# Six slots for streamed weights, other streamed pieces, and a row copied by one engine, in a recurrent memory transformer

## The chip, the cores and the metric

The kernel runs on one core of a Trainium2 chip. The metric is the device time of one execution in microseconds, as the median of several runs. A profiled execution gives a trace of every instruction and transfer; L448 is line 448 of the kernel file.

## The reference

Two independent parts are computed in bfloat16 and written side by side.

```python
def _A_ref(x, wqkv, wo):          # S = 2048, D = 640, 32 heads of 20
    ...                           # attention of each token to 8 tokens, 2 apart
def _B_ref(x, mem0, Wq, Wk, Wv, Wo, seg_len):
    ...                           # Dm = 640, H = 32, Dh = 192, M = 8, seg_len = 32
    for s in range(n_seg):        # 64 segments
        h = jnp.concatenate([mem, xs], axis=1)        # 8 + 32 = 40 rows
        q = jnp.einsum('btd,dhe->bhte', h, Wq)        # k, v the same
        ...
        p = _softmax(scores, axis=-1)
        o = jnp.einsum('bhqk,bhke->bhqe', p, v)
        o = jnp.einsum('bhte,hed->btd', o, Wo)
        mem = o[:, :M, :].copy()
        outs.append(o[:, M:, :])
```

In part B the first 8 rows of a segment's output are the memory of the next segment, so the 64 segments run one after the other.

## The kernel before

Part A runs first, for some 178 us. The text below is about part B.

**Weights in pieces.** Each of Wq, Wk and Wv is cut into 4 groups of 8 heads (1536 columns) and 5 chunks of 128 rows: a piece is named (group, chunk) and has 384 KB. Wo is cut into 24 output pieces of 320 KB, six to a group. Most pieces are resident in SBUF. Those listed in STREAMED (L258) are loaded anew in each segment: first copied to DRAM in a fitting layout (copy_streamed, L295), then, at each use, loaded by get_unit (L377) into one of `nbuf` slots of a rotating pool (wstream, 5 slots of 3072 bytes a partition). All these loads are issued by SP in the program's order. A load waits until TensorE has done the last matmul on the piece that was in its slot, that is, `nbuf` streamed pieces earlier. `pre` and `early` (L330, L363) say which resident pieces are loaded before, near the end of, and after part A.

**A segment** (L602) has a written order of TensorE's work: projections of Q and K by group, each followed by turns (transposes by a matmul with the identity, L465), scores (L521), softmax on VectorE and ScalarE (L526 to L538), values, mixing (L572), and the output projection (L586) that sums all heads into one PSUM tile Y. Rows of the next segments that are known beforehand are projected together with the present ones in some segments (RENEW, L261): a group's K or V pieces then get 8 matmuls each for 4.

**The order of a segment's pieces** as TensorE uses them: Q0, K0, Q1, K1, Q2, V0, K2, V1, output pieces 0 to 5, Q3, K3, V2, output 6 to 11, V3, output 12 to 17, three chunks of the late Q, output 18 to 23, two chunks of the late Q.

**The end of a segment** (L648 to L660): when Y is whole, `halves` (L458) copies its two halves to the bfloat16 tile `row`, the first by ScalarE (L459), the second by VectorE (L460). Both write one tile. TensorE finishes the late Q, whose result `halves` copies in the same way, turns the 8 memory rows (memory_rows, L590) from `row`, VectorE writes them into HX, the next segment's input (L600), and TensorE turns the late Q. The next segment's first projection reads HX. GpSimd stores `row` to the output (L659). The tile `row` shares its one buffer with the softmax tile t1 (L527) of the next segment.

`evacuate` (L426), which copies all other PSUM results, takes ScalarE and VectorE in turn.

Of the kernel before, what the change touches and what calls it, by code (L numbers as in the profile page):

```python
# [23 lines left out]
def part_a(ctx, tc, A_x, A_wqkv, A_wo, out, ident, emit_loads):  # L24
# [209 lines left out]
    with tc.manual_schedule(engines={mybir.EngineType.PE, mybir.EngineType.DVE, mybir.EngineType.Activation}):  # L234
# [5 lines left out]
        for b in range(n_blk):  # L240
# [14 lines left out]

STREAMED = {"k": ((0, 4), (0, 4), (0, 3), (0, 3)), "v": ((0, 1), (1,), (2,), (2,)),  # L258
            "o": (0, 4, 6, 8, 11, 14, 17, 18, 22, 23)}
SLOT = 1536  # L260
RENEW = {0: ("k0", "v2"), 1: ("k1", "v3"), 2: ("k2", "v0"), 3: ("k3", "v1")}  # L261
BLOCKS = 18
# [9 lines left out]
def part_b(ctx, tc, B_x, B_mem0, B_Wq, B_Wk, B_Wv, B_Wo, out, ident, n_seg, pre, nbuf, mid):  # L272
    nc = tc.nc
# [21 lines left out]
    def copy_streamed():  # L295
# [3 lines left out]
        for m, g in order:  # L299
            if m == "o":  # L300
                units += [("o", i, 0) for i in range(6 * g, 6 * g + 6) if i in STREAMED["o"]]
            else:
                units += [(m, g, dc) for dc in range(5) if m != "q" and dc in STREAMED[m][g]]
        for u in units:
# [6 lines left out]
    for m, g in need:  # L311
        if m == "o":
            resident += [("o", i, 0) for i in range(6 * g, 6 * g + 6) if i not in STREAMED["o"]]
        else:
            resident += [(m, g, dc) for dc in range(5) if m == "q" or dc not in STREAMED[m][g]]
    res, wait = {}, set()
# [113 lines left out]
    def load_x(s):  # L430
        if s < n_seg:
            nc.sync.dma_start_transpose(HXs[s % 2][:], XW[s])
# [4 lines left out]
    def ahead(s):  # L437
        return HXs[s % 2][:, :, SEG:2 * SEG]
# [16 lines left out]
        evacuate(sb[:], p[:])  # L455
        return sb

    def halves(dst, src, n):  # L458
        nc.scalar.copy(dst[:, 0:n], src[:, 0:n])  # L459
        nc.vector.tensor_copy(dst[:, n:], src[:, n:])  # L460

    def turn(sb):
        pt = ps_x.tile([128, 3, 4, 32], FP32, tag="x")
        for c in range(3):
            nc.tensor.matmul(pt[:, c], lhsT=sb[:, 128 * c:128 * c + 128], rhs=ident, start=True, stop=True)  # L465
        return pt
# [24 lines left out]
    def project_qk(s, m, g):  # L491
        renew = s == 0 or f"{m}{g}" in RENEW[s % 4]
        Xs = [ahead(s), main(s)] if renew else [main(s)]
        sbs = [to_sb(p) for p in project32(Xs, m, g)]

        def turns():
            if renew:
                turn_late(sbs[0], m, g, s, s)
            else:
                b = late.pop((m, g, s))  # L500
                fill(nc.gpsimd.tensor_copy, m, 32, L, b[:])
                free.append(b)
            fill(evacuate, m, 0, 32, turn(sbs[-1])[:])

        return turns

    def values(s, g):
        renew = s == 0 or f"v{g}" in RENEW[s % 4]
        ps = project32([ahead(s), main(s)] if renew else [main(s)], "v", g)
        for t, p in ((LV[g], ps[0]), (Vst, ps[-1]))[0 if renew else 1:]:  # L510
            v = t[:].rearrange("p (n e) -> p n e", e=64)
            w = bass.AP(v.tensor, v.offset, [v.ap[0], [256, 2], [1, 192]])
            evacuate(w, p[:].rearrange("p (h e) -> p h e", h=2))

    def scores(g):
        Sps = ps_x.tile([128, 4, L], FP32, tag="x")
        for n in range(8):
            a, part = n // 2, n % 2
            for g2 in range(2):
                at = L * (3 * a + g2 + part)  # L520
                nc.tensor.matmul(Sps[64 * g2:64 * g2 + 64, a, :], lhsT=QT[:, at:at + 64],  # L521
                                 rhs=KT[:, a, ((0, 1), (3, 2))[g2][part], :], start=(n == 0), stop=(n == 7),
                                 tile_position=(0, 64 * g2))
        return Sps

    def softmax(Sps):  # L526
        t1 = one.tile([128, 4, L], FP32, tag="t1")  # L527
        nc.vector.scalar_tensor_tensor(out=t1[:], in0=Sps[:], scalar=scale,  # L528
                                       in1=mask[:].unsqueeze(1).to_broadcast([128, 4, L]),
                                       op0=ALU.mult, op1=ALU.add)  # L530
        mx = small.tile([128, 4], FP32, tag="mx")
        nc.vector.tensor_reduce(out=mx[:], in_=t1[:], axis=AX.X, op=ALU.max)
        nc.vector.tensor_tensor(t1[:], t1[:], mx[:].unsqueeze(2).to_broadcast([128, 4, L]), op=ALU.subtract)  # L533
        nc.scalar.activation(t1[:], t1[:], ACTF.Exp)  # L534
        sm = small.tile([128, 4], FP32, tag="sm")
        nc.vector.tensor_reduce(out=sm[:], in_=t1[:], axis=AX.X, op=ALU.add)  # L536
        nc.vector.reciprocal(sm[:], sm[:])
        return t1, sm  # L538

    def put_p(s, g, t1, sm):  # L540
        i = s % 4
        if g == 0 and s:
            old = M * ((s - 1) % 4)
            nc.gpsimd.memset(P[:, 1, :, old:old + M], 0.0)
        for k, lo, hi, at in ((0, 0, 32, 0), (1, 32, L, M * i)):
            nc.vector.tensor_tensor(out=P[:, k, :, at:at + hi - lo], in0=t1[:, :, lo:hi],  # L546
                                    in1=sm[:].unsqueeze(2).to_broadcast([128, 4, hi - lo]), op=ALU.mult)

    def turn_p(split=1):

        pt = ps_x.tile([128, 2, 128], FP32 if split > 1 else BF16, tag="x")
        for late in range(2):
            src = P[:, late].rearrange("p a n -> p (a n)")
            if split == 1:
                nc.tensor.transpose(pt[:, late, :], src, ident)
                continue
            for h in range(2):
                nc.tensor.matmul(pt[64 * h:64 * h + 64, late, :], lhsT=src[:, 64 * h:64 * h + 64], rhs=ident,
                                 start=True, stop=True, tile_position=(0, 64 * h))
        PT = one.tile([128, 2, 2, L], BF16, tag="PT")  # L560
        evacuate(PT[:], pt[:].rearrange("p l (h n) -> p l h n", h=2)[:, :, :, 0:L])
        return PT
# [39 lines left out]
    def segment(s):  # L602
        last = s + 1 == n_seg
        load_x(s + 1)
        tq, tk, PT = {}, {}, {}
        tq[0] = project_qk(s, "q", 0)
        tk[0] = project_qk(s, "k", 0)
        tq[1] = project_qk(s, "q", 1)
        tq[0]()
        tk[0]()  # L610
        tk[1] = project_qk(s, "k", 1)
        put_p(s, 0, *softmax(scores(0)))
        tq[1]()
        tk[1]()
        tq[2] = project_qk(s, "q", 2)
        values(s, 0)
        soft = softmax(scores(1))
        tq[2]()
        PT[0] = turn_p()
        put_p(s, 1, *soft)  # L620
        tk[2] = project_qk(s, "k", 2)
        mix(0, PT[0])
        values(s, 1)
        tk[2]()
        PT[1] = turn_p()
        Y = ps_y.tile([128, 320], FP32, tag="y")
        project_out(Y, 0)
        put_p(s, 2, *softmax(scores(2)))
        tq[3] = project_qk(s, "q", 3)
        tk[3] = project_qk(s, "k", 3)  # L630
        mix(1, PT[1])
        values(s, 2)
        tq[3]()
        tk[3]()
        PT[2] = turn_p()
        project_out(Y, 1, range(0, 4))
        put_p(s, 3, *softmax(scores(3)))
        project_out(Y, 1, range(4, 6))
        mix(2, PT[2])
        values(s, 3)  # L640
        project_out(Y, 2, range(0, 4))
        PT[3] = turn_p(2)
        project_out(Y, 2, range(4, 6))
        mix(3, PT[3])
        if not last:
            gl = (s + 1) % 4
            ql = project32([ahead(s + 1)], "q", gl, range(0, 3))
        project_out(Y, 3)  # L648
        row = one.tile([128, 4, L], FP32, tag="t1")
        Ysb = row[:].rearrange("p a n -> p (a n)").bitcast(BF16)  # L650
        halves(Ysb, Y[:], 160)
        if not last:
            project32([ahead(s + 1)], "q", gl, range(3, 5), ql)
            sb = qk_sb.tile([128, 384], BF16, tag="sb", name="sb")
            halves(sb[:], ql[0][:], 192)
            memory_rows(s, Ysb)
            turn_late(sb, "q", gl, s, s + 1)
        for gv in range(2):
            nc.gpsimd.dma_start(out2[SEG * s:SEG * s + SEG, Dm + 320 * gv:Dm + 320 * gv + 320],  # L659
                                Ysb[64 * gv + M:64 * gv + L, :])  # L660
# [3 lines left out]
    with tc.manual_schedule(engines={mybir.EngineType.PE}):  # L664
        for s in range(n_seg):
            segment(s)


def run_all(ctx, tc, A_x, A_wqkv, A_wo, B_x, B_mem0, B_Wq, B_Wk, B_Wv, B_Wo, out, ident):
    n_seg = B_x.shape[1] // 32  # L670

    def mid(emit_loads):
        with ExitStack() as actx:
            part_a(actx, tc, A_x, A_wqkv, A_wo, out, ident, emit_loads)

    part_b(ctx, tc, B_x, B_mem0, B_Wq, B_Wk, B_Wv, B_Wo, out, ident, n_seg=n_seg, pre=110000, nbuf=5,
           mid=mid)


# [57 lines left out]
```

## Time and profile before

| what | us |
|---|---|
| median of 3 runs (2024.0 to 2032.36) | 2024.52 |
| the profiled execution | 2021.62 |
| its span, first to last instruction | 2019.8 |
| PE (TensorE matmul) busy | 1899.0 |
| DVE (VectorE) busy | 1226.9 |
| ACT (ScalarE) busy | 777.0 |

A line of groups names the line, engine, operation, the tiles written and read, the shape, the count, then busy time and mean ns of one. A line of waits names who waited for whom, the us in total, how often, and the longest. A line of windows has the stretch, its length, busy time with count of PE, PEld (weight loads), DVE, ACT and POOL, then the granted TensorE clock as a share of full speed, the DMA engines' mean busy share, and GB/s. A line of the timeline has start, length, engine, line and tiles, and in brackets the idle time before it with what ended that. SPq is the queue of SyncE, which issues transfers.

### The profile page before, as it was taken

The numbers are of one execution on the slowest core, as the hardware profiler recorded it, in microseconds if no ns is written. First come the engines' busy times: TensorE is split into PE (matmuls) and PEld (weight loads), VectorE is DVE, ScalarE is ACT, GpSimd is POOL, SyncE is SP. The second block draws the span as 40 slices with busy tenths as digits, with TensorE's granted clock in tenths as the row PEclk, the third lists the DMA queues.
The fourth block names the chain that finished last, engine by engine and source line by source line (L and its number), as shares of the span: only waits on it lengthen the run. The fifth ranks groups of instructions, "written<-read, shape, count | busy, mean of one in ns | idle before, by whom it ended". The sixth has DMA issues, their size and how long they took to land.

```text
span 2019.8 us, 98671 instructions
## 1 busy us (share of the span) xinstructions
PE 1899.0 (94%) x42640; PEld 1210.0 (60%) x42640; DVE 1226.9 (61%) x4041; ACT 777.0 (38%) x2480; POOL 259.3 (13%) x1058
## 2 busy tenths in 40 slices
PE   7998999999999999999999999999999999999998
PEld 3655566666666666566666565566655665556665
DVE  4876566655665656665566556555665565556565
ACT  3544333333333333333333333333333333334333
POOL 2000111111111111111111111111111111111111
PEclk9999999999999999999999999999999999999999
DMA  9927999999999999999899999999999998999997
GB/s 346 305 63 269 316 303 309 308 302 311 296 309 305 309 306 297 306 301 313 277 310 311 302 304 296 301 301 308 294 304 297 304 291 285 296 283 304 294 312 262
DMA packets 270134, 596.38 MB, mean 295 GB/s; under 512 B 61065, under 2 KB 72841, under 8 KB 269385
## 3 DMA queue, kind: packets, MB, share of 16 engines
q1 hardware_dynamic: 264770, 585.97, 88.0%
q8 instruction: 334, 5.47, 1.1%
q0 software_dynamic: 4928, 4.11, 0.6%
q14 instruction: 102, 0.84, 0.1%
HBM read 576.85 MB, written 18.87 MB: 295 GB/s over the span
## 4 chain that ended last, share of the span: by engine, by line
PE 55%; DMA 24%; DVE 15%; issue 3%; ACT 3%; SPq 0%; POOL 0%; DVEq 0%; ACTq 0%; POOLq 0%
PE acc L448 24%; PE Y L586 14%; DMA t<-wcopy_o 10%; DMA t<-wcopy_k 8%; PE pt L465 4%; PE pq L95 3%; PE Sps L521 3%; DMA out_dram<-row 3%; DMA t<-wcopy_v 2%; PE OTps L572 2%; DVE sb L428 2%; PE po L161 1%; DVE P L546 1%; DVE QT L428 1%; DVE sm L536 1%
## 5 line engine op out<-in xcount | busy, mean ns | idle before, releaser
L448 PEld LDWEIGHTS <-HX 128*32 128x32 bf16 x19380 | 466.2, 96 | 283.4 <-issue 50.6
L586 PEld LDWEIGHTS <-OT 128*64 128x64 bf16 x6144 | 319.8, 110 | 143.9 <-ACT OT L428 41.0
L586 PE MATMUL Y<-wres_o,OT 128*64 128x320 bf16 x3584 | 340.4, 300 | 4.1 <-ACT OT L428 1.3
L448 PE MATMUL acc<-wres_q,HX 128*32 128x384 bf16 x6460 | 335.8, 330 | 0.9 <-issue 0.3
L448 PE MATMUL acc<-t,HX 128*32 128x384 bf16 x4200 | 309.8, 329 | 15.1 <-DMA t<-wcopy_k 9.4
L586 PE MATMUL Y<-t,OT 128*64 128x320 bf16 x2560 | 280.9, 303 | 21.9 <-DMA t<-wcopy_o 20.3
L448 PE MATMUL acc<-wres_v,HX 128*32 128x384 bf16 x4844 | 277.0, 328 | 0.6 <-DVE OT L428 0.6
L448 PE MATMUL acc<-wres_k,HX 128*32 128x384 bf16 x3876 | 226.4, 328 | 0.6 <-issue 0.6
L428 DVE CAST sb<-acc 128x384 bf16<-128x384 f32 x291 | 160.9, 553 | 103.6 <-PE acc L448 87.1
L534 ACT ACTIVATE t<-t 128x160 f32<-128x160 f32 x256 | 86.2, 337 | 342.8 <-DVE t L533 341.0
L465 PE MATMUL pt<-ident,sb 128*128 128x128 bf16 x1938 | 190.5, 221 | 9.8 <-DVE sb L428 4.2
L428 ACT CAST sb<-acc 128x384 bf16<-128x384 f32 x292 | 138.8, 475 | 143.3 <-PE acc L448 136.3
L428 ACT CAST KT<-pt 64x128 bf16<-64x128 f32 (+3 forms) x517 | 139.3, 277 | 112.9 <-DVE KT L428 72.3
L465 PEld LDWEIGHTS <-sb 128*128 128x128 bf16 x1938 | 113.2, 97 | 89.6 <-issue 36.8
L528 DVE SCALAR_TENSOR_TENSOR t<-Sps,mask 128x160 f32<-128x160 f32 x256 | 82.9, 324 | 125.5 <-PE Sps L521 105.6
L428 ACT CAST OT<-OTps 128x120 bf16<-128x120 f32 x512 | 106.9, 261 | 126.5 <-PE OTps L572 125.0
L428 DVE CAST OT<-OTps 128x120 bf16<-128x120 f32 x512 | 125.5, 271 | 47.6 <-PE OTps L572 47.1
L428 DVE CAST KT<-pt 64x128 bf16<-64x128 f32 (+2 forms) x452 | 134.2, 300 | 31.1 <-ACT KT L428 23.0
L478 POOL COPY KT<-Lb 64x32 bf16<-64x32 bf16 x189 | 41.4, 219 | 825.1 <-PE Sps L521 825.1
L521 PEld LDWEIGHTS <-QT 128*64 128x64 bf16 x4096 | 100.3, 112 | 59.4 <-issue 50.3
L428 ACT CAST Vst<-acc 128x384 bf16<-128x384 f32 x205 | 98.7, 481 | 95.6 <-PE acc L448 92.0
L521 PE MATMUL Sps<-KT,QT 128*64 128x40 bf16 x4096 | 117.6, 187 | 9.2 <-DVE KT L428 6.2
(86 smaller groups left out, 1982.3 us busy)
## 6 DMA issues: line engine op xcount, KB each, us to landing
t<-wcopy_o SPq DMA_DIRECT2D x640, 320.0 KB, 4.3
t<-wcopy_k SPq DMA_DIRECT2D x512, 384.0 KB, 5.0
t<-wcopy_v SPq DMA_DIRECT2D x320, 384.0 KB, 4.8
wres_q<-in_B_Wq_dram SPq DMA_DIRECT2D x20, 384.0 KB, 7.7
wres_v<-in_B_Wv_dram SPq DMA_DIRECT2D x15, 384.0 KB, 7.7
wres_k<-in_B_Wk_dram SPq DMA_DIRECT2D x12, 384.0 KB, 7.7
wres_o<-in_B_Wo_dram SPq DMA_DIRECT2D x14, 320.0 KB, 7.6
wcopy_o<-in_B_Wo_dram SPq DMA_DIRECT2D x10, 320.0 KB, 9.4
```

The costliest lines, as they stand in the source:

```text
L95: nc.tensor.matmul(pq[32 * d:32 * d + 32], lhsT=wcol[:, k, t, 4 * c + d, :], rhs=xTs[s][:, k, :], start=(k == 0), stop=(k == 4), tile_posi ...
L161: nc.tensor.matmul(po[:, c % 2, :], lhsT=ident, rhs=prod[:, w, :], start=(w == 0), stop=(w == W - 1))
L428: (nc.scalar.copy if copies["n"] % 2 else nc.vector.tensor_copy)(dst, src)
L448: nc.tensor.matmul(ps[n][32 * j:32 * j + 32, :], lhsT=X[:, dc, :], rhs=w[:, 384 * j:384 * j + 384], start=(dc == 0), stop=(dc == 4), tile_ ...
L465: nc.tensor.matmul(pt[:, c], lhsT=sb[:, 128 * c:128 * c + 128], rhs=ident, start=True, stop=True)
L478: copy(KT[64:128, :, 3, n0:n1], src[64:128, 1])
L521: nc.tensor.matmul(Sps[64 * g2:64 * g2 + 64, a, :], lhsT=QT[:, at:at + 64], rhs=KT[:, a, ((0, 1), (3, 2))[g2][part], :], start=(n == 0), s ...
L528: nc.vector.scalar_tensor_tensor(out=t1[:], in0=Sps[:], scalar=scale, in1=mask[:].unsqueeze(1).to_broadcast([128, 4, L]), op0=ALU.mult, op ...
L534: nc.scalar.activation(t1[:], t1[:], ACTF.Exp)
L536: nc.vector.tensor_reduce(out=sm[:], in_=t1[:], axis=AX.X, op=ALU.add)
L572: nc.tensor.matmul(ps[a][:, k, :], lhsT=V[32 * a:32 * a + 32, col:col + 128], rhs=PT[32 * a:32 * a + 32, late, half, :], start=(n == 0), s ...
L586: nc.tensor.matmul(Y[64 * gv:64 * gv + 64, :], lhsT=OT[:, L * c:L * c + 64], rhs=w[:, n:n + 320], start=(i == 0 and r == 0), stop=(i == 23 ...
```

## The change

Six slots stand for five. The lists of streamed pieces are new: as many K and output pieces as before, and six V pieces for five. The resident set is smaller by that V piece, as the pool of slots is larger by one. `halves` is gone; ScalarE copies Y, and the late Q, each in one instruction.

```diff
-STREAMED = {"k": ((0, 4), (0, 4), (0, 3), (0, 3)), "v": ((0, 1), (1,), (2,), (2,)),
-            "o": (0, 4, 6, 8, 11, 14, 17, 18, 22, 23)}
+STREAMED = {"k": ((2, 4), (2, 4), (0, 4), (0, 4)), "v": ((0, 4), (0, 4), (2,), (2,)),
+            "o": (3, 5, 7, 10, 11, 13, 17, 18, 22, 23)}
...
-    def halves(dst, src, n):
-        nc.scalar.copy(dst[:, 0:n], src[:, 0:n])
-        nc.vector.tensor_copy(dst[:, n:], src[:, n:])
...
-        halves(Ysb, Y[:], 160)
+        nc.scalar.copy(Ysb, Y[:])
...
-            halves(sb[:], ql[0][:], 192)
+            nc.scalar.copy(sb[:], ql[0][:])
...
-    part_b(ctx, tc, B_x, B_mem0, B_Wq, B_Wk, B_Wv, B_Wo, out, ident, n_seg=n_seg, pre=110000, nbuf=5,
+    part_b(ctx, tc, B_x, B_mem0, B_Wq, B_Wk, B_Wv, B_Wo, out, ident, n_seg=n_seg, pre=110000, nbuf=6,
```

The orders of instructions on TensorE, VectorE, ScalarE and GpSimd stay as they are, but for the copies named and the tiles that hold a piece. On SP the 64 added loads come in, the transposing load of HX stands one streamed load later, and at the start of part B the first six streamed loads go ahead of the early resident pieces.

## Prediction

> **What bounds the kernel now.** I read the page first: shares of the span, the chain that ended last, the transfers.
>
> ```profile
> span 2019.8 us, 98671 instructions
> ...
> PE 1899.0 (94%) x42640; PEld 1210.0 (60%) x42640; DVE 1226.9 (61%) x4041; ACT 777.0 (38%) x2480; POOL 259.3 (13%) x1058
> ...
> PE 55%; DMA 24%; DVE 15%; issue 3%; ACT 3%; SPq 0%; POOL 0%; DVEq 0%; ACTq 0%; POOLq 0%
> ...
> L428 ACT CAST sb<-acc 128x384 bf16<-128x384 f32 x292 | 138.8, 475 | 143.3 <-PE acc L448 136.3
> ...
> L428 ACT CAST OT<-OTps 128x120 bf16<-128x120 f32 x512 | 106.9, 261 | 126.5 <-PE OTps L572 125.0
> ...
> t<-wcopy_o SPq DMA_DIRECT2D x640, 320.0 KB, 4.3
> t<-wcopy_k SPq DMA_DIRECT2D x512, 384.0 KB, 5.0
> t<-wcopy_v SPq DMA_DIRECT2D x320, 384.0 KB, 4.8
> ```
>
> TensorE is busy 94% of the span, so at most 120 us can be won by letting it wait less. The chain goes through streamed weights for a quarter of the span: DMA is TensorE's partner at the limit. Per segment 10 + 8 + 5 = 23 pieces are streamed (640, 512 and 320 over 64 segments). Next I asked what TensorE waits for, then what the SP queue, which starts these transfers, waits for.
>
> ```profile
> PE Y L586 <- DMA t<-wcopy_o: 20.3, 41, 1.5
> PE pt L597 <- DVE row L460: 19.9, 63, 0.4
> PE acc L448 <- DMA t<-wcopy_k: 9.4, 22, 1.4
> ...
> PE acc L448 <- DMA t<-wcopy_v: 2.7, 7, 0.6
> ```
>
> ```profile
> SPq L394 <- PE acc L448: 681.7, 771, 4.0
> SPq L394 <- PE Y L586: 279.0, 352, 2.5
> ```
>
> TensorE waits 32.4 us (70 times, mean 0.46) for streamed pieces, and 19.9 us for the row. SP in its turn spends 961 us in these two rows alone waiting until TensorE gives a slot back. Transfers thus start late for want of a slot. Is DMA also full? The windows of the trace compare the loading phase, where transfers are issued without slots, with two ordinary segments:
>
> ```profile
> 20.00:30.00 10.00, 10.00 (x188) 6.79 (x180) 3.67 (x3) 4.71 (x9) 0.00 (x0) 1.00 1.03 406
> ...
> 780.00:837.00 57.00, 54.77 (x1276) 34.94 (x1273) 34.47 (x122) 21.42 (x72) 7.64 (x32) 1.00 0.93 302
> ```
>
> The last column is GB/s: 406 there, 302 here. The column before it, DMA's busy share, is near 1 in both, so it doesn't tell how much more could be moved; GB/s does.
>
> The length of a segment comes from the transposes of the memory rows, one set per segment, first and last start in the row: (1988.6 - 218.9) / 62 = 28.54 us.
>
> ```profile
> L597 PE MATMUL pt<-ident,row x378: 166/173/194, 218.9 to 1988.6; 128*128 128x8 bf16 x126, 128*64 128x8 bf16 x63
> ```
>
> **Change 1: slots and pieces.** The new lists stream 8 K, 6 V and 10 output pieces: the added one is a V piece. A segment then moves 14 x 384 + 10 x 320 = 8576 KB (8.78 MB) for 8192; the extra 384 KB take 0.97 us of DMA at 406 GB/s. SP issues one more transfer, and it waits most of the time as it is.
>
> What a slot allows is its cycle. Five slots and 23 pieces: each slot is filled once in 28.54 x 5 / 23 = 6.20 us. Six and 24, at a segment of 27.8: 6.95 us. From issue to landing of a piece:
>
> ```profile
> DMA to landing us min/median/max: 2.9/4.7/7.9
> ```
>
> So 1.50 us is left for waiting in the slot and being read, and 2.25 after: 0.75 more on average. Placement decides where the slack is short. Prices for counting it, from the chain in order of time in one segment:
>
> ```profile
> 900.07 1.74 PE acc L448 x40
> 901.81 0.36 PE Sps L521 x16
> ...
> 908.59 1.75 PE Y L586 x24
> ```
>
> A projection piece of four matmuls is 0.17 us, an output piece 0.29, scores 0.36. In the old order, output piece 11 takes the slot of K piece (3, 0), five pieces back. Between them lie four pieces of K 3 (0.70), mix, five pieces of V 2 (0.87), turns, output pieces 6 to 10 (1.46) and scores, about 4 us: under the median landing. In the new order its slot is that of output piece 5; scores 2 and the five pieces of Q 3 come in addition (+0.36 and +0.87), so 5.2. The tightest place is now V piece (3, 2), six back from which stands K (3, 0): the old 4 us, output 11, mix and two pieces of V 3, about 4.9. Everywhere the distance is at or above the median landing; before, it wasn't.
>
> Price of a wait: besides the idle time that the view shows, it loses the overlap of matmuls. One lasts 299 ns, while 24 of them go by in 1.75 us, 73 ns each; 0.23 us per wait, so 32.4 + 70 x 0.23 = 48.5 us.
>
> ```profile
> L586 PE MATMUL Y<-t,OT x2560: 296/299/323, 198.4 to 2014.2; 128*64 128x320 bf16 x197
> ```
>
> How much of it goes? Bounds: all 48.5, or nothing, if the sixth transfer only queues behind the five. With waits of 0.46 us on average I take them as exponentially spread. The 0.75 us shrink where pieces are queued back to back, since the sixth lands 0.97 us behind the fifth; I take 0.45 net. What stays is exp(-0.45 / 0.46) = 38%, so **30 us** go.
>
> **The clock.** The last output piece, 23, has the longest waits, and they come where TensorE soon waits for the row as well. Three windows of 3.4 us before and at such a place, and the wait in the first:
>
> ```profile
> 978.60:982.00 3.40, 1.98 (x33) 0.96 (x36) 0.87 (x4) 0.85 (x3) 0.90 (x2) 1.00 0.84 309
> 982.00:985.40 3.40, 3.40 (x51) 1.77 (x47) 0.49 (x2) 0.72 (x2) 0.36 (x2) 0.50 0.90 296
> ...
> 1787.50:1790.90 3.40, 3.39 (x43) 1.64 (x47) 0.92 (x4) 0.96 (x3) 1.25 (x3) 0.51 1.02 389
> ...
> 1876.30:1879.70 3.40, 3.40 (x48) 1.81 (x44) 0.99 (x3) 0.72 (x2) 0.00 (x0) 0.50 0.98 356
> ```
>
> ```profile
> 979.66 0.46 PE L586 MATMUL Y<-t,OT 128*64 128x320 bf16 x4 [1.29 <-DMA t<-wcopy_o]
> ```
>
> The seventh column is the granted clock: 0.5 for 3.4 us, three times, 1.7 us each. Piece 23 took the slot of V piece (3, 2) and now takes that of output piece 11, a mix and three V pieces (0.52) earlier, so I let these go: **5 us** (bounds 0 and 5). The Trainium skill, "TensorE: Matmul & The Clock Gate", section Part 1, has the clock fall to half after an idle window of about 3.4 us; a wait of 1.3 us would cost no clock then, and this term would be nothing. In the trace the clock fell after 3.4 us in which TensorE was busy for 1.98, so I keep the 5.
>
> **Change 2: the row and the late Q by ScalarE alone.** The end of an ordinary segment in order of time:
>
> ```profile
> 866.96 0.29 ACT L459 CAST row<-Y 128x160 bf16<-128x160 f32 x1 [2.38 <-PE Y L586]
> 867.29 0.33 DVE L460 CAST row<-Y 128x160 bf16<-128x160 f32 x1 [2.67 <-ACT row L459]
> 867.42 0.32 ACT L459 CAST sb<-acc 128x192 bf16<-128x192 f32 x1 [0.16 <-PE acc L448]
> 867.67 0.38 PE L597 MATMUL pt<-ident,row 128*64 128x8 bf16 x6 [0.30 <-DVE row L460]
> 867.77 0.36 DVE L460 CAST sb<-acc 128x192 bf16<-128x192 f32 x1 [0.15 <-ACT sb L459]
> 867.91 0.56 PE L465 MATMUL pt<-ident,sb 128*128 128x128 bf16 x3
> 868.09 0.20 DVE L600 CAST HX<-pt 128x40 bf16<-128x40 f32 x1
> 868.40 1.00 PE L448 MATMUL acc<-wres_q,HX 128*32 128x384 bf16 x20
> ```
>
> The halves don't run side by side: VectorE's starts when ScalarE's has ended, so the row takes 866.96 to 867.62, 0.66 us. One ScalarE copy of 320 columns lies between 261 ns (120) and 475 (384): 0.42. The transposes start at 867.44 for 867.67, which their wait of 0.30 allows; HX is written by 868.06 for 868.29. The late Q is copied behind the row, 867.41 to 867.89 (475 ns), and its three turns follow at 867.94, done in time for the next projection at 868.17 for 868.40. That is 0.23 us in each of 63 segments, **14.5 us**. If the longer copy of Q held up the turns by 0.1, it would be 8; above, no more than the wait of 19.9. ScalarE, busy 38%, hides the extra; what is late next is the copy into HX.
>
> **Change 3: the start.** In the changed kernel's order of issue six streamed pieces go ahead of the last nine early resident pieces, and four stores of part A stand before these.
>
> ```profile
> 163.64 2.00 SPq L394 DMA_DIRECT2D t<-wcopy_k  x4
> 165.68 0.76 SPq L394 DMA_DIRECT2D t<-wcopy_v  x1
> 169.44 9.52 SPq L176 DMA_DIRECT2D out_dram<-ob  x4
> 179.33 1.50 SPq L328 DMA_DIRECT2D wres_v<-in_B_Wv_dram  x1
> ```
>
> Before, one early piece was behind the stores that end at 178.96; now five are, four more or 3.9 us of DMA inside segment 0. One streamed piece is earlier, and that segment lasts 39 us with its doubled projections, so most is hidden: I take **1 us lost** (bounds 0 and 4).
>
> **Sum.** 30 + 5 + 14.5 - 1 = 48.5 us. The profiled execution took 2021.62 us (its span 2019.8 and 1.8 around it), so it would take 1973.1. The median of the three runs shown, 2024.52, lies 2.9 above that execution, and the changed kernel will be measured by such a median: 1976.
>
> **Rivals.**
> All waits go: 18.5 more and the start costs nothing: 1956. For it speaks that 0.75 us exceed the mean wait; against it, landings of up to 7.9 us.
>
> The store of the row takes over. The next segment's first softmax writes into the row's buffer, so it waits for that store:
>
> ```profile
>   DMA out_dram<-row: 9.2, 11
> ```
>
> Waits for K pieces early in a segment then only turn into this one. With half of the 30 us lost that way or to the new clusters: 1991.
>
> The sixth slot does nothing, the added piece eating it: 14.5 - 1, so 2011, about no gain.
>
> The other side: DMA is full at 302 GB/s, as its share of 0.93 would have it. Then 8.78 MB take 29.1 us, 0.53 over today's segment, 63 times 33 us, less the row's 14.5 and plus the start: 2044. It decides as soon as the sustained rate is under 8.78 MB / 28.54 us = 308 GB/s. The 406 speaks against it, the share for it. The Trainium skill, "DMA: Bandwidth & Descriptors", section Bandwidth, puts the limit of HBM for one core at about 358 GB/s; by that a segment needs 24.5 us of transfers, an estimate, and the rival fails too. The trace's 406 lies above that figure.
>
> **How the numbers follow.** Forecast 0.46, all gone 0.20, half 0.18, nothing from the slot 0.08, DMA full 0.08. The range from 1948 to 2012 holds the forecast, the third case, four fifths of the second and half of the fourth, 0.84; its low end is 8 us under the second case, for waits shorter than the lost overlap, which no view of waits shows. A measurement can tell about 0.5%, 10 us, from no change: under 2014 is faster. The first three cases are faster, and 0.03 of the fourth: 0.87. Same are the rest of the fourth and 0.01 of the last, 0.06; slower is the rest of the last, 0.07.
>
> **What would show it.** In the changed profile: TensorE's waits for streamed pieces near 12 us instead of 32.4; landings about as now, near 5; the row's wait near 0.1 us each time; no half clock around piece 23; segments of 27.8 us; over 310 GB/s. Landing medians of 6 and more would mean that DMA is full; waits for the row's store well over 9 us would mean the second rival.

## The result and the profile after

The changed kernel takes 1999.64 us (median of 4 runs, 1996.27 to 2006.95), the kernel before 2028.44 (4 runs, 2024.0 to 2033.85): a ratio of 0.9862, 95% interval 0.9818 to 0.9905. A second measurement (e5 below) gave 0.9897 (0.9869 to 0.9925). The gain is thus some 20 to 29 us, about half of the 48.5 that were forecast, and inside the range. The profiled executions are 2021.62 us before and 2006.95 after, 14.7 apart; the latter is the slowest of its four, so what the two traces show in single terms is read against 14.7.

From the page of the changed kernel: span, busy time, chain, transfers.

```profile
span 2005.2 us, 98676 instructions
...
PE 1896.5 (95%) x42640; PEld 1211.5 (60%) x42640; DVE 1184.5 (59%) x3914; ACT 794.9 (40%) x2480; POOL 259.0 (13%) x1058
...
PE 60%; DMA 16%; DVE 15%; issue 4%; ACT 4%; POOL 1%; SPq 0%; DVEq 0%; ACTq 0%; POOLq 0%
...
t<-wcopy_o SPq DMA_DIRECT2D x640, 320.0 KB, 4.7
t<-wcopy_k SPq DMA_DIRECT2D x512, 384.0 KB, 5.3
t<-wcopy_v SPq DMA_DIRECT2D x384, 384.0 KB, 5.4
```

DMA's share of the chain falls from 24% to 16%. The median landing of each kind is up by 0.3 to 0.6 us: six transfers are under way where five were. The window of two segments that the prediction showed with 302 GB/s is now:

```profile
780.00:837.00 57.00, 53.63 (x1258) 34.33 (x1255) 33.08 (x118) 21.05 (x71) 7.74 (x32) 1.00 0.98 314
```

The chain by line shows the one DMA term that grew, the store of the row; before, then after:

```profile
PE acc L448 24%; PE Y L586 14%; DMA t<-wcopy_o 10%; DMA t<-wcopy_k 8%; PE pt L465 4%; PE pq L95 3%; PE Sps L521 3%; DMA out_dram<-row 3%; DMA t<-wcopy_v 2%; PE OTps L572 2%; DVE sb L428 2%; PE po L161 1%; DVE P L546 1%; DVE QT L428 1%; DVE sm L536 1%
PE acc L448 24%; PE Y L582 18%; DMA out_dram<-row 7%; PE pt L461 4%; PE pq L95 3%; DMA t<-wcopy_o 3%; DMA t<-wcopy_k 3%; PE OTps L568 3%; PE Sps L517 3%; DVE sb L428 2%; DMA t<-wcopy_v 2%; DVE t L524 2%; DVE P L542 2%; PE po L161 1%; DVE mx L528 1%
```

What TensorE waits for, in the changed kernel:

```profile
PE Sps L517 <- DVE KT L428: 11.3, 30, 0.5
...
PE acc L448 <- issue: 7.3, 13, 1.8
PE Y L582 <- DMA t<-wcopy_o: 6.8, 12, 2.0
...
PE acc L448 <- DMA t<-wcopy_k: 4.2, 9, 1.2
PE OTps L568 <- issue: 3.0, 6, 0.9
PE acc L448 <- DMA t<-wcopy_v: 3.0, 5, 1.4
...
PE Y L582 <- issue: 0.9, 1, 0.9
...
PE pt L461 <- issue: 0.3, 1, 0.3
```

Streamed pieces now cost 14.0 us in 26 waits for 32.4 in 70, and the wait for the row is gone from the view. New is "issue", time in which TensorE waits for nothing that the profile shows: 11.5 us in 21 waits. Before it was 1.6. The waits for VectorE's copies of K, the first line, have grown as well:

```profile
PE Sps L521 <- DVE KT L428: 6.2, 16, 0.4
...
PE acc L448 <- issue: 0.9, 2, 0.6
PE OTps L572 <- issue: 0.5, 1, 0.5
...
PE pt L465 <- issue: 0.2, 1, 0.2
```

The tile of softmax and streamed weights, in the changed kernel: VectorE's waits for the row's store (us, times; 9.2 and 11 before), and the landings.

```profile
  DMA out_dram<-row: 19.9, 18
...
DMA to landing us min/median/max: 3.2/5.1/7.7
```

The end of a segment, changed kernel, in order of time:

```profile
866.56 0.43 ACT L647 CAST row<-Y 128x320 bf16<-128x320 f32 x1 [2.04 <-PE Y L582]
867.01 0.48 ACT L651 CAST sb<-acc 128x384 bf16<-128x384 f32 x1
...
867.04 0.39 PE L593 MATMUL pt<-ident,row 128*64 128x8 bf16 x6
...
867.46 0.20 DVE L596 CAST HX<-pt 128x40 bf16<-128x40 f32 x1 [2.91 <-PE pt L593]
...
867.55 0.34 PE L461 MATMUL pt<-ident,sb 128*128 128x128 bf16 x3
...
867.82 0.67 PE L448 MATMUL acc<-wres_q,HX 128*32 128x384 bf16 x12
```

From the row's copy to the next projection it is 1.26 us, before 1.44 (866.96 to 868.40): 0.18 less; over all 63 segments the medians are 1.26 and 1.43. The copy of the row takes 0.43, and HX is written by 867.66; it is now the three turns of the late Q, which wait for its whole copy, that end last.

The memory rows' transposes, with the first segment's end at 221.9 (218.9 before):

```profile
L593 PE MATMUL pt<-ident,row x378: 166/173/193, 221.9 to 1973.4; 128*128 128x8 bf16 x126, 128*64 128x8 bf16 x63
```

A segment takes (1973.4 - 221.9) / 62 = 28.25 us, where 27.8 was forecast and 28.54 was the time before.

### The profile page after: what moved, and what is told of

Its sections match the earlier page's. It is cut to its first block, busy times and chain, and to the rows that moved or that the text cites. A ratio compares the mean times of both kernels' runs of the same rounds, so it can differ in the third digit from the quotient of the medians.

```text
span 2005.2 us, 98676 instructions
## 1 busy us (share of the span) xinstructions
PE 1896.5 (95%) x42640; PEld 1211.5 (60%) x42640; DVE 1184.5 (59%) x3914; ACT 794.9 (40%) x2480; POOL 259.0 (13%) x1058
## 4 chain that ended last, share of the span: by engine, by line
PE 60%; DMA 16%; DVE 15%; issue 4%; ACT 4%; POOL 1%; SPq 0%; DVEq 0%; ACTq 0%; POOLq 0%
PE acc L448 24%; PE Y L582 18%; DMA out_dram<-row 7%; PE pt L461 4%; PE pq L95 3%; DMA t<-wcopy_o 3%; DMA t<-wcopy_k 3%; PE OTps L568 3%; PE Sps L517 3%; DVE sb L428 2%; DMA t<-wcopy_v 2%; DVE t L524 2%; DVE P L542 2%; PE po L161 1%; DVE mx L528 1%
## 5 line engine op out<-in xcount | busy, mean ns | idle before, releaser
L448 PE MATMUL acc<-t,HX 128*32 128x384 bf16 x4524 | 346.1, 328 | 10.5 <-DMA t<-wcopy_k 4.2
L582 PE MATMUL Y<-wres_o,OT 128*64 128x320 bf16 x3584 | 332.6, 303 | 2.9 <-ACT OT L428 0.3
L582 PE MATMUL Y<-t,OT 128*64 128x320 bf16 x2560 | 268.5, 302 | 8.6 <-DMA t<-wcopy_o 6.8
L448 PE MATMUL acc<-wres_v,HX 128*32 128x384 bf16 x4520 | 254.3, 328 | 5.1 <-issue 4.0
L461 PE MATMUL pt<-ident,sb 128*128 128x128 bf16 x1938 | 179.6, 222 | 14.7 <-DVE sb L428 4.8
L517 PE MATMUL Sps<-KT,QT 128*64 128x40 bf16 x4096 | 120.9, 187 | 16.1 <-DVE KT L428 11.3
```

The costliest lines, as they stand in the source:

```text
L448: nc.tensor.matmul(ps[n][32 * j:32 * j + 32, :], lhsT=X[:, dc, :], rhs=w[:, 384 * j:384 * j + 384], start=(dc == 0), stop=(dc == 4), tile_ ...
L582: nc.tensor.matmul(Y[64 * gv:64 * gv + 64, :], lhsT=OT[:, L * c:L * c + 64], rhs=w[:, n:n + 320], start=(i == 0 and r == 0), stop=(i == 23 ...
```

## The experiments

Three readings were to be told apart: that the terms of the forecast hold and something new eats the rest; that the added V piece and its traffic eat it; that the row's term is worth less than 14.5 us.

### e1: the row alone

```diff
-STREAMED = {"k": ((2, 4), (2, 4), (0, 4), (0, 4)), "v": ((0, 4), (0, 4), (2,), (2,)),
-            "o": (3, 5, 7, 10, 11, 13, 17, 18, 22, 23)}
+STREAMED = {"k": ((0, 4), (0, 4), (0, 3), (0, 3)), "v": ((0, 1), (1,), (2,), (2,)),
+            "o": (0, 4, 6, 8, 11, 14, 17, 18, 22, 23)}
...
-    part_b(ctx, tc, B_x, B_mem0, B_Wq, B_Wk, B_Wv, B_Wo, out, ident, n_seg=n_seg, pre=110000, nbuf=6,
+    part_b(ctx, tc, B_x, B_mem0, B_Wq, B_Wk, B_Wv, B_Wo, out, ident, n_seg=n_seg, pre=110000, nbuf=5,
```

> Five slots and the old list of pieces, with only the row and the late Q copied by ScalarE alone. The part's own worth: the prediction had 0.23 us per segment, 14.5 us in all; in the trace of the changed kernel the stretch from the last output piece to the next segment's first projection is 0.18 us shorter (1.60 for 1.77), so this theory expects 11 us under the kernel before. Rival: with five slots an earlier segment start only makes TensorE wait longer for the first K pieces, so less than 4 us are left.

Measured: a ratio of 0.9983 (0.9959 to 1.0007), 3.4 us under the kernel before, by the interval anything from nothing to 8 us: the 11 us of the theory are excluded, and the rival fits. The end of a segment is as much shorter as in the changed kernel, but TensorE's waits are:

```profile
PE Y L582 <- DMA t<-wcopy_o: 25.9, 45, 1.4
PE acc L448 <- DMA t<-wcopy_k: 15.9, 33, 1.7
...
PE acc L448 <- DMA t<-wcopy_v: 4.2, 9, 0.9
```

46.0 us in 87 waits for 32.4 in 70. With five slots a TensorE that is ready sooner waits longer: the waits grew by 13.6 us, more than the 11 that the end of the segments gives. So the rate at which slots come round seems to set the pace.

### e2: slots and list alone

```diff
-        nc.scalar.copy(Ysb, Y[:])
+        halves(Ysb, Y[:], 160)
...
-            nc.scalar.copy(sb[:], ql[0][:])
+            halves(sb[:], ql[0][:], 192)
```

> Six slots and the new list, but row and late Q still copied in two halves. If the parts add up, the changed kernel's gain of 29 us less the row's 11: 18 us under the kernel before. Rival: the row's gain is only there because the pieces are on time; then the slots alone give nearly all, 25 us or more.

Measured: 0.9944 (0.9920 to 0.9968), 11.3 us. Neither number fits well; it is below both. Between this and the changed kernel's two ratios lie 10 to 17 us, the worth of the row when there are six slots, for 3.4 with five. That the two parts need each other is likely by this, not shown: the intervals are wide, and the profiled executions don't have the difference (spans of 2005.5 us here, 2005.2 and 2005.7 in the changed kernel's two).

### e3: the new list with five slots

```diff
-    part_b(ctx, tc, B_x, B_mem0, B_Wq, B_Wk, B_Wv, B_Wo, out, ident, n_seg=n_seg, pre=110000, nbuf=6,
+    part_b(ctx, tc, B_x, B_mem0, B_Wq, B_Wk, B_Wv, B_Wo, out, ident, n_seg=n_seg, pre=110000, nbuf=5,
```

> The changed kernel with five slots: the new list with its added piece, without the sixth slot. A slot's cycle falls from 28.54 x 5 / 23 = 6.20 us to 5.95, so TensorE waits for streamed pieces more than the kernel before's 32 us, some 50, and the time is 5 to 25 us above the kernel before in spite of the row. Rival: the new places do the work and the slot little; then the time is near the changed kernel's, 20 us or more under the kernel before.

Measured: 1.0227 (1.0191 to 1.0262), 46 us slower than before, more than expected. TensorE's waits for streamed pieces are 72.5 us in 161:

```profile
PE Y L582 <- DMA t<-wcopy_o: 32.9, 76, 1.1
PE acc L448 <- DMA t<-wcopy_k: 21.3, 46, 1.3
PE acc L448 <- DMA t<-wcopy_v: 18.3, 39, 2.1
```

The median landing was 4.7 us as in the kernel before, so DMA wasn't slower. It is the slot that makes the gain. The list by itself brings none; how much of its loss is the added piece and how much the places, this run doesn't tell.

### e4: the old list with six slots

```diff
+ALIAS = {('v', 3, 4): ('v', 3, 3)}
...
+    resident = [u for u in resident if u not in ALIAS]
...
     def get_unit(u):
+        u = ALIAS.get(u, u)
```

> Six slots with the old list of 23 pieces; the space comes from V piece (3, 4), which is not loaded: chunk 3's weights are used twice. If the added piece and its 25 MB of traffic ate part of the gain (later landings, a later store of the row, late instructions), this is 8 to 20 us faster than the changed kernel, 37 to 49 us under the kernel before, with landings near 4.7 us. Rival: the added traffic costs nothing and the missing gain has another cause; then it is within 5 us of the changed kernel.

Measured: 0.9782 (0.9747 to 0.9817), 44 us under the kernel before. Waits for streamed pieces are 5.6 us in 15. The added piece, which the smaller resident set makes necessary, and the places that go with it cost 16 to 23 us of what the sixth slot gives (0.9782 for 0.9862 and 0.9897). But "issue" stays, 12.6 us in 18 waits, and so does the store, 22.8 us: these two don't come from the added piece alone.

### e5: the changed kernel again

> The changed kernel once more, beside the next three on the same chip. If the six slots are what lets the row's 11 us through (alone the row gave 3), it lies 20 to 33 us under the kernel before, and its trace again has some 10 us of TensorE waits that nothing in the profile explains ('issue') and some 20 us of VectorE waits for the row's store. Rival: its first four runs were lucky and the parts simply add up; then 11 to 18 us under the kernel before.

Measured: 0.9897 (0.9869 to 0.9925), 20.8 us, at the lower end; "issue" 11.3 us, the store 20.5 us.

### e6: six pieces less to stream

```diff
-STREAMED = {"k": ((2, 4), (2, 4), (0, 4), (0, 4)), "v": ((0, 4), (0, 4), (2,), (2,)),
-            "o": (3, 5, 7, 10, 11, 13, 17, 18, 22, 23)}
+STREAMED = {"k": ((2,), (2,), (0,), (0,)), "v": ((0, 4), (0,), (2,), (2,)),
+            "o": (3, 5, 7, 10, 13, 17, 18, 22, 23)}
+ALIAS = {("v",1,4):("v",1,3), ("k",0,4):("k",0,3), ("k",1,4):("k",1,3), ("k",2,4):("k",2,3), ("k",3,4):("k",3,3), ("o",11,0):("o",9,0)}
```

> The changed kernel with six streamed pieces (chunk 4 of every K group and of V 1, output piece 11) neither streamed nor loaded; a resident neighbour's weights are used twice. TensorE runs the same instructions, DMA moves 2.2 MB per segment less, some 240 GB/s. Theory: the 'issue' waits of TensorE (11.5 us in the changed kernel, 1.6 before) come when the loading of instructions is held up by the streamed traffic; then they fall under 4 us, and the time is 1960 us or less. Rival: they come because TensorE, no longer held up by streamed pieces, outruns the loading of its instructions; then they stay at 10 us or more with this much less traffic, and the time is near 1975.

Measured: 0.9664 (0.9643 to 0.9685), 1951.36 us. Some 8 us of this are a shorter start, since six pieces needn't be copied: part B begins at 170.8 us for 179.2 in e5. All of TensorE's waits for "issue" that are left, and in a second view the store's and the landings:

```profile
PE acc L451 <- issue: 2.0, 3, 1.0
```

```profile
  DMA out_dram<-row: 28.5, 29
...
DMA to landing us min/median/max: 2.7/4.0/7.7
```

No wait for a streamed piece is left, and yet "issue" falls to 2.0 us: it isn't a faster TensorE that makes it, but the traffic. Instructions come by DMA too; this line of the page is the same in both kernels but for its share:

```profile
q8 instruction: 334, 5.47, 1.2%
```

334 packets of 16 KB, one for each 256 of the 85,529 instructions that the trace has of TensorE, matmuls and weight loads above all. Numbered in order of time, all 21 "issue" waits of the changed kernel fall on an instruction whose number leaves 193 to 195 when divided by 256, and so do all 242 in the 14 traces of this case: the waits are for the next block of TensorE's instructions. The nine of the changed kernel that are over 0.5 us end 1.3 to 1.6 us after the end of such a packet.

With five slots "issue" costs 1.6 us (before) and 0.8 (e1) with 23 pieces and 5.3 with 24 (e3); with six, 12.6 with 23 (e4), 11.5 and 11.3 with 24, 2.0 with 18. The other kernels with six slots and 24 pieces have 10.0 to 17.5. So it goes with the slots and the traffic. Eight of the nine packets took 0.9 to 1.4 us themselves, and the median of all is 1.0: the delay lies ahead of their transfer. Whether they waited in a queue or were asked for late wasn't tried.

The Trainium skill, "Runtime: NRT & Kernel Launch", section Instruction fetch mechanics, has instructions fetched in blocks of 16 KiB, 256 instructions each, while the block before is executed, and the cost of passing from block to block mostly hidden. The size and the 256 agree; hidden the cost is here only as long as the streamed weights leave room.

The store's waits, on the other hand, rise to 28.5 us with less traffic. The store doesn't land later (5.3 us in the median, as in the changed kernel); so the next softmax must be ready sooner.

### e7: a buffer of its own for the row

```diff
-        row = one.tile([128, 4, L], FP32, tag="t1")
+        row = one.tile([128, 4, L], FP32, tag="row")
...
+ALIAS = {('o', 21, 0): ('o', 20, 0)}
```

> The changed kernel with a buffer of its own for the row, so that the next segment's softmax doesn't wait for the row's store; the space comes from output piece 21, which is not loaded: piece 20's weights are used twice. Theory: the store is a bound that took over as the streamed pieces came on time; VectorE's 19.9 us of waits for it go, and 8 to 20 us of time. Rival: the chain behind it (scores, softmax, the turn of P) or the next streamed piece is as late anyway, and less than 4 us are won.

Measured: 0.9793 (0.9764 to 0.9822), 1978.66 us, 22.7 under the changed kernel beside it. The wait for the store is gone. Streamed pieces cost 17.8 us and "issue" 11.2, much as in e5 (15.2 and 11.3). The store is thus a bound of its own. Some 1 us of the 22.7 is a shorter start (the first memory rows are turned at 219.1 us for 220.3). TensorE meets the store by way of VectorE, whose softmax and all that it does behind it come late: the waits for VectorE's copies of K, 9.7 us in e5, are back at the kernel before's value.

```profile
PE Sps L520 <- DVE KT L431: 6.3, 16, 0.4
```

### e8: the store by ScalarE's queue

```diff
-            nc.gpsimd.dma_start(out2[SEG * s:SEG * s + SEG, Dm + 320 * gv:Dm + 320 * gv + 320],
+            nc.scalar.dma_start(out2[SEG * s:SEG * s + SEG, Dm + 320 * gv:Dm + 320 * gv + 320],
```

> The changed kernel with the row's store issued by ScalarE's queue for GpSimd's. If the store lands sooner so (5.3 us from issue to landing now; under 4.5), VectorE's waits for it fall under 5 us and the time by 5 to 15 us. Rival: issuing takes ScalarE's time at the segment's start, where it copies the late Q's turns and the first projections, and the time stays or rises by up to 15 us.

Measured: 0.9897 (0.9861 to 0.9932), 1996.42 us for 2001.39 of the changed kernel: no difference that can be told. Both theories hold at once. VectorE's waits for the store fall to 3.8 us, by the earlier issue and the later segment behind it, since the landing takes 5.1 us as ever. But the issue stands between ScalarE's two copies:

```profile
868.19 0.42 ACT L647 CAST row<-Y 128x320 bf16<-128x320 f32 x1 [1.84 <-PE Y L582]
868.64 0.32 ACTq L655 DMA_DIRECT2D out_dram<-row  x1
...
869.00 0.48 ACT L651 CAST sb<-acc 128x384 bf16<-128x384 f32 x1 [0.39 <-ACT row L647]
```

The copy of the late Q starts 0.81 us after the row's, for 0.45 in the changed kernel, and the next segment with it: from the row's copy to the next projection it is 1.62 us for 1.26, in the median of 63 segments.

### e9: the store on two queues

```diff
-            nc.gpsimd.dma_start(out2[...], Ysb[64 * gv + M:64 * gv + L, :])
+            (nc.gpsimd, nc.sync)[gv].dma_start(out2[...], Ysb[64 * gv + M:64 * gv + L, :])
```

> The changed kernel with the second half of the row's store issued by SP for GpSimd, so that it needn't wait 0.5 us behind the first half's issue. With a buffer of its own the row's store cost nothing and 23 us were won; the same theory expects VectorE's waits for the store to fall from 20 to under 10 us here and 5 to 15 us of time. Rival: SP stands in front of the row while slots come free behind it, streamed pieces land later, TensorE's waits for them rise over 20 us, and the time stays.

Measured: 0.9861 (0.9827 to 0.9894), 1996.12 us. The store's waits fall from 20 us to 3.8, as the theory had it. Those for streamed pieces rise from 15.2 to 20.5, as the rival had it, and the gain over the changed kernel (0.9862 and 0.9897) isn't clear of the intervals.

### e10 and e11: another list, and that list with e9's store

```diff
-STREAMED = {"k": ((2, 4), (2, 4), (0, 4), (0, 4)), "v": ((0, 4), (0, 4), (2,), (2,)),
-            "o": (3, 5, 7, 10, 11, 13, 17, 18, 22, 23)}
+STREAMED = {"k": ((0, 3, 4), (0, 4), (0, 2), (0, 4)), "v": ((0,), (0, 4), (3,), (3,)),
+            "o": (0, 5, 6, 8, 10, 15, 17, 18, 21, 23)}
```

> The changed kernel with a list of 9 K, 5 V and 10 output pieces: the added piece is a K piece at the segment's start, and of the output pieces 22 and 23, 10 and 11 that follow each other directly only one each is streamed, so no piece is wanted sooner than 0.8 us after the one before. If crowded places are what is left of the waits for streamed pieces (14 us and their lost overlap), they fall to about 7 us and the time by 5 to 15 us. Rival: the waits come from late landings by chance, wherever the pieces stand, and stay at 12 us or more.

> Both together, the whole computation kept. If the two are bounds of their own, their gains add: 10 to 30 us under the changed kernel, 1970 to 1990 us. Rival: what one gives back the other takes, as the row's 11 us were taken with five slots; then no better than the better of the two alone.

Measured: e10 0.9962 (0.9939 to 0.9986), e11 0.9941 (0.9918 to 0.9964); both worse than the changed kernel, against either expectation. The waits of e10:

```profile
PE acc L448 <- DMA t<-wcopy_k: 36.2, 58, 1.4
```

The list isn't what was expected of it. Five K pieces are wanted at the segment's start, and (0, 3) and (0, 4) directly after each other, four matmuls or 0.17 us apart and not 0.8; counted along the trace, (0, 4) has 33 of the 58 waits and 20.4 us of them. The transposing load of HX, too, stands in SP's queue among the five. K piece (0, 4) lands 5.7 us after its issue and (1, 4) 6.4 in the median, only 0.3 and 0.4 more than the same pieces in the changed kernel, while output pieces take 4.1 to 5.4. The crowding is thus the likelier cause, the queue in front a smaller one; the two weren't tried apart. Since the list is itself crowded, the run doesn't test its theory. In e11 the store's waits are gone (0.8 us), but the K pieces' stay at 33.2.

### e12: other places after the middle alone

```diff
-STREAMED = {"k": ((2, 4), (2, 4), (0, 4), (0, 4)), "v": ((0, 4), (0, 4), (2,), (2,)),
-            "o": (3, 5, 7, 10, 11, 13, 17, 18, 22, 23)}
+STREAMED = {"k": ((2, 4), (2, 4), (0, 4), (0, 3)), "v": ((0, 4), (0, 4), (4,), (3,)),
+            "o": (3, 4, 7, 10, 11, 12, 17, 18, 21, 23)}
```

> The whole computation, with the store on two queues and the changed kernel's list but for seven pieces after the segment's middle: K 3 chunk 3 for 4, V 2 chunk 4 for 2, V 3 chunk 3 for 2, output pieces 4, 12 and 21 for 5, 13 and 22. The start of the segment stays as in the changed kernel. Where a slot is given back earlier or a piece is wanted later, TensorE's waits for V and output pieces should fall from 12 us (store on two queues, old places) to 6 or less, and the time by 4 to 10 us under that kernel: a ratio near 0.982 to the kernel before. Rival: places in the second half do not matter, since landings scatter; waits and time stay, a ratio of 0.986.

Measured: 0.9847 (0.9818 to 0.9876), 1991.06 us. Waits for V and output pieces are 8.1 us for e9's 12.1, for all streamed pieces 13.2 for 20.5. The direction is the expected one, the size less, and the step from e9 lies inside both intervals. Of the kernels that compute everything it has the lowest time, though not clear of e9's.

## Why the prediction was half right

**Slots and pieces: right.** Waits for streamed pieces went from 32.4 us in 70 to 14.0 in 26; with 0.23 us of lost overlap each that is 48.5 to 20.0, so 28.5 us for the forecast 30 (24.8 by e5, 15.2 us in 37). Output piece 23 alone went from 10.6 us in 19 waits to 2.6 in 5. The 0.23 us are the prediction's estimate; no run measures them by themselves. The view said near 12 us of waits and landings near 5; they are 14.0 and 5.1. DMA was not full at 302 GB/s: the same window of the changed kernel has 314, and loading phases 406. The slot is the gain, as e3 shows. That the new places were good isn't shown: the new list loses in e3, and against e4, with its added piece in it. That places matter is shown by e10; e12's better ones are not clear of the intervals.

**The added piece: underpriced.** The prediction counted it in the slot's cycle and in 0.97 us of DMA. e4 without it, and with the old places, is some 20 us faster; which of the two it is stays open.

**The row: right in mechanism, and conditional.** 0.18 us per segment, 11 us, for the forecast 0.23 and 14.5. The row itself came 0.23 sooner (0.43 us for 0.66), as worked out; what failed is "its three turns follow, done in time": the next projection came 0.33 us after the end of the late Q's copy (867.49), not 0.28. More important, the sum took the term as independent of the slots. With five it is worth 3.4 us, at most 8 (e1).

**The clock: wrong.** No half clock stands at piece 23 of an ordinary segment any more. But it fell as often elsewhere, once after an "issue" wait of 1.83 us; two windows of 3.4 us there, TensorE busy for 1.57 in the first:

```profile
1565.90:1569.30 3.40, 1.57 (x58) 0.76 (x54) 1.98 (x9) 0.76 (x3) 0.75 (x4) 1.00 0.88 253
1569.40:1572.80 3.40, 3.40 (x31) 2.13 (x28) 0.32 (x1) 0.48 (x1) 0.12 (x1) 0.51 0.79 216
```

Between the start and the end of part B each trace has four windows of 3.4 us at half clock: nothing for the forecast 5 us.

**The start: mechanism right, size off.** Segment 0 ends 3.0 us later (221.9 for 218.9), for 1 forecast with 4 as the bound; in e5's trace segment 1 begins 1.5 us later (221.1 for 219.5). Most of what the 3.0 has more is a half clock (0.50 granted from 217.8 to 221.2 us, up to 1.7 us lost) that e5 lacks there. The segment lasts 41 us (178.1 to 219.5 before), not 39, which changes nothing. The early pieces do go behind part A's stores.

**What was missing.** 28.5 + 11 - 3 = 36.5 us; the traces are 14.7 apart. Of the 22 between, "issue" is 11.5 - 1.6 = 9.9 us of idle time and 17 more waits at 0.23, together 13.8, a mechanism that the prediction didn't have at all. The rest, 8 us, fits the store, whose waits rose from 9.2 to 19.9 us: TensorE's waits for VectorE's copies of K rose from 6.2 us in 16 to 11.3 in 30, 5.1 us and 14 more at 0.23, together 8.3, and e7 without the store's wait has 6.3 in 16. That was the second rival, with a chance of 0.18: it was priced as half of the streamed term lost, and e7 shows that without the store's wait the changed kernel is some 22 us faster. The account is of one execution, the slowest of four, and rests on the estimate of 0.23 us a wait; that it comes out so closely is in part luck.

The forecast took the likeliest course as one in which all terms add. The store was seen in the row "9.2, 11" and made a rival, though a bound that is already reached in 11 of 63 segments is likely to be reached more often when what stands in front of it gets shorter. All that was missing pointed one way; the range held the time because the rivals had widened it, not because the likeliest course came.

## What to carry to other kernels

Where transfers wait for slots, a faster engine gains little (here 3 us of 11), and one more slot may let the saving count: price the two together, and pay for the slot with as little new traffic as can be. Before summing what a removed wait returns, list the waits that end just before it in the same stretch (here a store that holds a shared buffer, some 22 us); they take over. Keep streamed pieces that are used directly after each other apart, and look at what stands in the transfer queue ahead of each.

## What was not expected of the hardware

With the transfer queue kept fuller TensorE waits for its own instructions, always at the same place in a block of 256: 1.6 us with five slots, 11.5 with six, 2.0 with six slots and a quarter less streamed weight (e6: 6336 KB per segment for 8576).

The store of 20 KB takes 4.9 to 5.4 us to land by GpSimd's, ScalarE's or SP's queue alike, with 243 GB/s of traffic (e6) or with 314. Only an earlier issue brought it forward.

The half clock set in after 3.4 us in which TensorE was busy for 1.5 to 2.1 us, in all seven cases of the two kernels' part B, though none of the waits in them was over 2 us. It doesn't always: from 1746.6 to 1750.0 us of the kernel before TensorE was busy for 1.86, and the clock stayed full.
